# Four tokens a partition for the first four blocks of a gated-linear-attention and squared-ReLU kernel, with small array tiles and per-operation ranks

## The chip, the cores and the metric

One Trainium2 chip (trn2), one of its cores. The metric is device time in microseconds (us) of one execution. The runs of the kernel before within one job here lie 1.4 to 3.8% apart, so a comparison is always made with runs of the kernel before on the same chip in the same rounds. A run counts as slow when it is over 1.5% above the fastest run of its kernel, and else as fast. The ratio given is the mean time of one kernel's fast runs over the mean of the other's fast runs of the same rounds, with a 95% interval; it is therefore not quite the ratio of the medians quoted beside it. A "span" is the length of the one profiled execution; it is some 1.7 us shorter than that execution's time. In the views of the profile PE is TensorE (PEld its weight loads), DVE VectorE, ACT ScalarE, POOL GpSimd and SP SyncE; L701 is line 701 of that run's kernel.

## The reference

```python
def _attn_ref(q, k, v, alpha):            # (4, 8, 768, 48) each
    state = zeros((B, H, D, D))
    for t in range(S):
        state = alpha[:, :, t, :, None] * state + einsum('bhd,bhe->bhde', k[:, :, t], v[:, :, t])
        y[:, :, t] = einsum('bhd,bhde->bhe', q[:, :, t], state)

def _moe_ref(x, w_in, w_out, s, b):       # x (3072, 384), w_in (384, 2048), w_out (2048, 384)
    h = x @ w_in
    g = s * maximum(h, 0) ** 2 + b
    return g @ w_out
```

The attention runs over 24 blocks of 128 tokens. For each block there are a cumulative sum of log alpha, scores under a mask, a state product and the output of the block (`y`). Then come the first product (`h`), ReLU, square, and the second product. The constant `b` becomes one row, b times the column sums of `w_out`, which a small "bias matmul" makes once all of `w_out` has landed; the second product's results cannot be finished before.

## The kernel before

A small list scheduler orders all operations from modelled durations and ranks, and they are emitted in that order, so each engine has a fixed row of work. The parts that matter here:

```python
    h_ps = [ps.tile([128, 512], FP32, name=f"h_ps{i}") for i in range(2)]     # two tiles
    o_ps = [ps.tile([128, 512], FP32, name=f"o_ps{i}") for i in range(2)]
...
    def mm1(w):                                  # one unit of the first product
        hp = h_ps[w % 2]
        for i, j in enumerate(js):
            for kk in range(3):
                nc.tensor.matmul(out=hp[:, i * n : (i + 1) * n],
                                 lhsT=w_in_bf[:, kk, 128 * j : 128 * (j + 1)],
                                 rhs=xd_sb[g % 3][:, kk, 0:n], start=(kk == 0), stop=(kk == 2))

    def relu(w):
        nc.scalar.activation(out=r_sb[w % 2], in_=h_ps[w % 2], func=AF.Relu)
...
    def st_yevac(n):                             # output of a block, PSUM to the input of the first product
        dst, src = xd_sb[g % 3][:, :, t * C : (t + 1) * C], y_of(n)
        if n < 2 * NR2:                          # blocks loaded as pairs: tokens come in another order
            dst = dst.rearrange("a k (p j) -> a k j p", j=2)
            src = src.rearrange("a k (j p) -> a k j p", j=2)
        nc.scalar.activation(out=dst, in_=src, func=AF.Copy)
...
    def fill(idle, at):                          # keeps TensorE active in the gaps that the model sees
        for _ in range(int((idle - FILL_GAP) / (0.44 if at < COLD else 0.22))):
            nc.tensor.matmul(out=o_ps[0], lhsT=zeros[:, 0:128], rhs=zeros, start=True, stop=True)
```

While TensorE fills one `h_ps` tile (a named buffer; `ps` lies in PSUM, where TensorE writes its results), ScalarE reads the other.

## Time and profile before

| | before |
|---|---|
| time, median (range) of the 4 runs beside the changed kernel | 188.42 us (186.82 to 189.61) |
| span of the profiled execution | 183.4 us |
| first matmul of the first product | 16.99 us |
| end of the bias matmul | 38.33 us |
| rest of the span after it | 145.1 us |

The last two rows are the sum that the prediction works with. The prediction shows the page, the windows and the chain. Three groups, with shapes kept apart: line, engine, operation, tiles, shapes and count; then busy us and mean ns of one; then the engine's idle time just before and what ended it.

```profile
L692 PE MATMUL h_ps<-xd,w_in_bf 128*128 128x256 bf16 x528 | 67.7, 273 | 0.1
L701 ACT ACTIVATE r<-h_ps 128x512 bf16<-128x512 f32 x96 | 56.3, 604 | 30.3 <-PE h_ps L692 22.8 <-DVE gt L707 3.6 <-DVE am L498 1.2
L672 ACT ACTIVATE xd<-o_ps 128x384 bf16<-128x384 f32 x2 | 1.2, 600 | 1.8 <-PE o_ps L527 1.8
```

The chain (start, us, what):

```profile
131.72 0.34 PE py_ps L527 x16
132.06 1.42 PE h_ps L692 x12
133.48 0.65 PE o_ps L754 x4
```

### The profile page before, as it was taken

Reading aid. Unit: us, or ns where it says so; the run is one execution under the profiler, and the core shown is the slowest. Engines: PE = TensorE matmul, PEld = TensorE weight load, DVE = VectorE, ACT = ScalarE, POOL = GpSimd, SP = SyncE. Lnnn points to the kernel's source line nnn. Section 1 sums busy time; section 2 is a strip of 40 time slices with the busy share of each in tenths; the row PEclk is TensorE's granted clock in tenths of the full one; section 3 lists DMA queues with packets and bytes.
Section 4 is the critical chain, followed back from the end, with each engine's and each line's share of the span. In section 5 each row is a group of like instructions: output and inputs, shape, how many; then the busy total and the mean of one; then the engine's idle time right before and its main releaser. Section 6 shows DMA issues by size and latency. Waiting matters only on the chain.

```text
span 183.4 us, 5324 instructions
## 1 busy us (share of the span) xinstructions
PE 174.6 (95%) x2133; PEld 124.2 (68%) x2135; DVE 138.7 (76%) x255; ACT 106.0 (58%) x215; POOL 40.2 (22%) x70
## 2 busy tenths in 40 slices
PE   6988896999999999999999999999999999999993
PEld 2356574767777776676776776776876776777762
DVE  2377999999899898687789688577897788544421
ACT  3437699946676565674764754853753662665400
POOL 7995032022112423110303311101230131000000
PEclk9999999999999999999999999999999999999999
DMA  5999999999999999996998979996974994101112
GB/s 154 355 295 321 361 370 323 193 178 223 201 185 199 214 183 192 205 211 156 228 169 178 211 153 215 185 228 146 210 175 103 209 194 119 46 4 43 43 43 86
DMA packets 115816, 34.42 MB, mean 188 GB/s; under 512 B 109008, under 2 KB 114256, under 8 KB 115792
## 3 DMA queue, kind: packets, MB, share of 16 engines
q1 hardware_dynamic: 98832, 29.89, 69.2%
q10 hardware_dynamic: 16896, 4.20, 15.7%
q8 instruction: 16, 0.26, 0.6%
q14 instruction: 8, 0.07, 0.1%
q0 software_dynamic: 64, 0.00, 0.0%
HBM read 25.17 MB, written 4.72 MB: 163 GB/s over the span
## 4 chain that ended last, share of the span: by engine, by line
PE 79%; DVE 8%; SPq 6%; DMA 4%; issue 1%; DVEq 0%
PE o_ps L754 32%; PE h_ps L692 31%; PE py_ps L527 5%; SPq L217 5%; PE a_ps L489 4%; DMA gt<-in_k_dram 4%; PE ct_ps L386 2%; DVE colpart L342 2%; DVE gt L707 1%; SPq L309 1%; PE ct_ps L447 1%; PE ct_ps L433 1%; DVE colsum L347 1%; DVE qk L589 1%; PE o_ps L723 1%
## 5 line engine op out<-in xcount | busy, mean ns | idle before, releaser
L692 PE MATMUL h_ps<-xd,w_in_bf 128*128 128x256 bf16 (+1 forms) x624 | 74.4, 265 | 0.1
L701 ACT ACTIVATE r<-h_ps 128x512 bf16<-128x512 f32 x96 | 56.3, 604 | 30.3 <-PE h_ps L692 22.8
L754 PE MATMUL o_ps<-w_out_bf,gt 128*128 128x384 bf16 x368 | 69.5, 326 | 1.4 <-ACT w_out_bf L318 1.3
L692 PEld LDWEIGHTS <-w_in_bf 128*128 128x128 bf16 x624 | 55.1, 97 | 11.1 <-issue 0.4
L707 DVE TENSOR_TENSOR gt<-r 128x512 bf16<-128x512 bf16 x96 | 42.7, 456 | 19.5 <-ACT r L701 18.4
L754 PEld LDWEIGHTS <-gt 128*128 128x128 bf16 x368 | 34.6, 98 | 19.4 <-issue 1.5
L498 DVE TENSOR_TENSOR am<-a_ps,mask 128x1024 bf16<-128x1024 f32 x24 | 29.3, 1221 | 2.3 <-PE a_ps L489 2.0
L483 POOL TENSOR_TENSOR s_st<-s_st,blast 128x384 bf16<-128x384 bf16 x16 | 14.6, 914 | 63.7 <-DVE s_st L472 46.0
L410 POOL CAST vp<-v_in 128x384 bf16<-128x384 f32 x20 | 12.2, 608 | 47.7 <-DMA v_in<-in_v_dram 40.7
L672 ACT ACTIVATE xd<-py_ps 128x384 bf16<-128x384 f32 x22 | 11.0, 502 | 17.8 <-PE py_ps L527 15.9
L765 DVE SCALAR_TENSOR_TENSOR o_sb<-o_ps,s_col,bias_w 128x384 f32<-128x384 f32 x23 | 14.2, 616 | 6.0 <-PE o_ps L754 5.0
L380 ACT ACTIVATE la<-a_in 128x384 bf16<-128x384 f32 x20 | 10.4, 521 | 7.3 <-DVE gt L707 4.5
L416 DVE TENSOR_TENSOR qk<-q_in,b_s 128x384 bf16<-128x384 f32 x20 | 12.5, 627 | 0.8 <-ACT b_s L402 0.7
L421 DVE TENSOR_TENSOR qk<-k_in,binv 128x384 bf16<-128x384 f32 x20 | 11.9, 596 | 0.1
L402 ACT ACTIVATE b_s<-ct_ps 128x384 f32<-128x384 f32 x20 | 9.7, 486 | 2.6 <-PE ct_ps L386 2.2
L405 ACT ACTIVATE binv<-ct_ps 128x384 f32<-128x384 f32 x20 | 9.9, 495 | 0.0
L489 PE MATMUL a_ps<-qkT 64*128 64x128 bf16 x192 | 9.5, 219 | 0.4 <-DVE am L498 0.2
L489 PEld LDWEIGHTS <-qkT 64*128 64x128 bf16 x192 | 5.5, 94 | 6.5 <-issue 5.1
L1026 PE MATMUL o_ps<-zeros 128*128 128x512 bf16 x19 | 7.7, 551 | 1.3 <-DVE zeros L235 1.3
L527 PE MATMUL py_ps<-am,vp 128*32 128x128 bf16 x352 | 8.8, 219 | 0.0
L472 DVE TENSOR_TENSOR s_st<-ct_ps,s_st 64x192 bf16<-64x192 f32 x20 | 7.0, 352 | 2.0 <-PE ct_ps L447 1.6
L527 PEld LDWEIGHTS <-vp 128*32 128x32 bf16 x384 | 6.5, 97 | 0.9 <-issue 0.6
(95 smaller groups left out, 133.4 us busy)
## 6 DMA issues: line engine op xcount, KB each, us to landing
out_dram<-o_sb SPq DMA_DIRECT2D x23, 192.0 KB, 2.5
v_in<-in_v_dram SPq DMA_DIRECT2D x20, 192.0 KB, 3.8
a_in<-in_alpha_dram SPq DMA_DIRECT2D x20, 192.0 KB, 4.1
k_in<-in_k_dram SPq DMA_DIRECT2D x20, 192.0 KB, 4.0
q_in<-in_q_dram SPq DMA_DIRECT2D x20, 192.0 KB, 3.9
wst<-in_moe_w_in_dram SPq DMA_DIRECT2D x4, 768.0 KB, 7.5
gt<-in_moe_w_out_dram SPq DMA_DIRECT2D x4, 768.0 KB, 9.2
gt<-in_alpha_dram SPq DMA_DIRECT2D x2, 384.0 KB, 4.9
```

What stands on the lines that cost most here:

```text
L410: nc.gpsimd.tensor_copy(out=vp_sb[n % 4].rearrange("a p (x d) -> a p x d", d=D)[:, :, 0:3:2, :], in_=v_in[n % NIN].rearrange("a (p e) d -> ...
L416: nc.vector.tensor_tensor(out=qk_sb[n % 4][:, 0, :, 0:D], in0=q_in[n % NIN], in1=b_sb[n % 2], op=ALU.mult)
L421: nc.vector.tensor_tensor(out=qk_sb[n % 4][:, 1, :, 0:D], in0=k_in[n % NIN], in1=binv_sb[n % 2], op=ALU.mult,)
L483: nc.gpsimd.tensor_tensor(out=s_sb[n % 3], in0=t1_sb[n % 2], in1=bl, op=ALU.mult)
L489: nc.tensor.matmul(out=a_ps[:, e, p, :], lhsT=qkT[64 * e : 64 * e + 64, 1, p, :], rhs=qkT[64 * e : 64 * e + 64, 0, p, :], start=True, stop ...
L498: nc.vector.tensor_tensor(out=am_sb[n % 2].rearrange("a e p t -> a (e p) t"), in0=a_ps.rearrange("a e p t -> a (e p) t"), in1=(mask2 if n ...
L527: nc.tensor.matmul(out=y_of(n)[32 * (x % 4) : 32 * (x % 4) + 32, x // 4, :], lhsT=(st[:, p, c0 : c0 + 32] if e is None else vp[:, p, c0 + ...
L692: nc.tensor.matmul(out=hp[:, i * n : (i + 1) * n], lhsT=w_in_bf[:, kk, 128 * j : 128 * (j + 1)], rhs=xd_sb[g % 3][:, kk, 0:n], start=(kk = ...
L701: nc.scalar.activation(out=r_sb[w % 2], in_=h_ps[w % 2], func=AF.Relu)
L707: nc.vector.tensor_tensor(out=gt_sb[:, s0 : s0 + m, js[0] : js[0] + len(js)].rearrange("a s j t -> a j s t"), in0=r, in1=r, op=ALU.mult,)
L754: nc.tensor.matmul(out=op[:, 0:d_model], lhsT=gt_sb[:, s0, j], rhs=w_out_bf[:, j, :], start=(j == 0), stop=(j == NJ - 1),)
L765: nc.vector.scalar_tensor_tensor(out=ots, in0=o_ps[(x // 4) % 2][:, 0:d_model], scalar=s_col, in1=bias_w, op0=ALU.mult, op1=ALU.add,)
```

## The change

Intent: the first four blocks, which before were loaded as two pairs with two tokens a partition (384-byte pieces), are loaded as one quad with four tokens a partition (768-byte pieces). V is brought into order by 32-row array tiles, the state products of these blocks run on 32 rows, and every early operation has a rank of its own. `NPE` is the number of blocks that TensorE transposes; the others go to transposing DMAs. The core of the diff (the table of some 200 ranks, renamings and the scheduler's bookkeeping are cut):

```diff
-GROUPS = [2, 2, 1, 1, 2, 2, 2, 2, 2, 2, 2, 2, 2]
+GROUPS = [2, 2, 2, 2, 2, 2, 2, 2, 2, 2, 2, 2]
-NPE = 8
+NPE = 6
...
-TC2 = ["DVE", "DVE"]
-CE = ["POOL", "DVE", "ACT", "ACT", "ACT", "ACT", "ACT", "ACT"]
+R = 4
+TC2 = ["ACT", "ACT", "ACT", "DVE"]
+A2 = [0, 1, 0, 0]
+CE = ["POOL", "ACT", "DVE", "POOL", "ACT", "POOL", "ACT", "ACT"]
...
-    h_ps = [ps.tile([128, 512], FP32, name=f"h_ps{i}") for i in range(2)]
+    hh_ps = ps.tile([128, 2, 512], FP32, name="hh_ps")
+    h_ps = [hh_ps[:, i] for i in range(2)]
...
+            in_=src[0, :, 0 : R * C, :].rearrange("h (s j) d -> s h (j d)", j=R),
...
+    def a_of(n):
+        return hh_a if n < R and A2[n] else a_ps
...
+    def quad_vshift(c):                  # 4 matmuls on 32 x 32 array tiles a block
+            nc.tensor.matmul(out=v4_ps[c][RC * j : RC * j + RC, 0 : H * D], lhsT=ident_bf[r, r], ...
+                tile_position=(RC * c, RC * j))
...
     def st_yevac(n):
+        if n < R:
+            dst = dst.rearrange("a k (p j) -> a k j p", j=R)
+            src = src.rearrange("a k (j p) -> a k j p", j=R)
...
     def fill(idle, at):
-        for _ in range(int((idle - FILL_GAP) / (0.44 if at < COLD else 0.22))):
+        for _ in range(int((idle - FILL_GAP) / (0.11 if at < COLD else 0.06))):
-                out=o_ps[0], lhsT=zeros[:, 0:128], rhs=zeros, start=True, stop=True
+                out=o_ps[0][:, 384:512], lhsT=zeros[:, 0:128], rhs=zeros[:, 0:128], start=True, stop=True
```

The two lines with `hh_ps`: during the start-up the same tile (the "two-bank tile" of the expectations, which call 512 FP32 columns a bank) also serves, as one view, for cumulative sums and for one block's scores.

## The prediction

> **What bounds the kernel now.** I read the page first (busy shares, 40 slices), then a table of windows, then the chain that ended last, then the groups with shapes kept apart, from which all durations below come.
>
> ```profile
> PE   6988896999999999999999999999999999999993
> DVE  2377999999899898687789688577897788544421
> DMA  5999999999999999996998979996974994101112
> GB/s 154 355 295 321 361 370 323 193 178 223 201 185 199 214 183 192 205 211 156 228 169 178 211 153 215 185 228 146 210 175 103 209 194 119 46 4 43 43 43 86
> ```
>
> One slice is 183.4/40 = 4.585 us. TensorE looks full nearly everywhere, but in the first eight slices that is partly filler and gaps. So I cut the span where the work changes:
>
> ```profile
> 10.00:18.00 8.00, 6.59 (x116) 4.64 (x115) 6.29 (x10) 4.62 (x9) 5.77 (x10) 1.00 1.03 305
> 18.00:28.00 10.00, 8.97 (x121) 6.49 (x120) 9.76 (x16) 8.42 (x14) 1.50 (x2) 1.00 1.07 366
> 28.00:38.30 10.30, 8.90 (x89) 6.18 (x89) 10.19 (x19) 9.83 (x17) 1.00 (x1) 1.00 0.99 237
> 38.30:60.00 21.70, 21.70 (x356) 16.25 (x354) 20.46 (x38) 13.50 (x33) 4.39 (x7) 1.00 0.97 201
> 60.00:100.00 40.00, 40.00 (x502) 28.73 (x499) 33.87 (x65) 23.95 (x54) 8.72 (x11) 1.00 1.13 194
> ```
>
> Columns: window, length, then busy us and count of PE, weight loads, DVE, ACT and POOL, granted clock, DMA share, GB/s. From 18 to 38.3 VectorE (9.76 of 10, 10.19 of 10.3) and, in its second half, ScalarE (9.83) have no room, while TensorE has holes. From 38.3 on TensorE is full. The chain says the same:
>
> ```profile
> 11.76 6.75 DMA gt<-in_k_dram
> 19.08 1.82 DVE qk L589 x2
> ...
> 29.46 1.50 DVE colpart L342
> ...
> 34.48 0.87 DVE colpart L342
> ...
> 36.83 0.54 DVE colsum L350
> 37.41 0.91 PE o_ps L367 x2
> 38.33 0.65 PE h_ps L692 x6
> ```
>
> Columns: start, us, what. The K load of the second pair landed at 18.5; then VectorE in one run to the last fold of the column sums at 37.4; then the bias matmul; then TensorE alone to 180.35, and about 3 us for the last two stores. So the model is: span = (end of the bias matmul) + (TensorE work ordered after it) + (its small gaps) + 3.05.
>
> Check of that model on this kernel. In program order after the bias matmul stand 74 first-product units of 6 x 256 columns and 8 of 12 x 128 (0.65 and 0.67 us each in the chain), 88 second-product quads (0.65; the last four run as a split tail of 2.66), 20 score groups (0.33), 17 + 20 output parts (0.17 and 0.34), 4 transposes (0.45), 19 cumulative sums (0.17) with 15 last-row parts (0.18), 16 state products (0.17). That is 140.3 us. Measured: 180.35 - 38.33 = 142.0. The model leaves 1.7 us of gaps in all the rest.
>
> [...] its granted-clock column stays at 1.00: the first 384-column matmuls, at 5.0 us, start 0.3 apart; the same four at 16.1 us start 0.165 apart. [...] The pair loads move 384 B pieces, yet the second slice, all pairs, shows 355 GB/s against 361 and 370 in the slices of 1.5 to 2 KB weight rows: at most 4% to win on 3.1 MB. [...] The before kernel has 64-row products (0.34 us for eight) beside full ones and shows no gap that I can assign to it.
>
> **The change part by part.** (1) Two pairs become one quad. Per-instruction work on the muls is unchanged: 4 of 128x768 before (0.95 to 1.1), 4 now. Four pair transposition copies on DVE at 0.68 become one on DVE and three on ACT. An ACT pass costs 0.81 at 768 and 1.48 at 1536 columns, so 1.04 at 1024 (estimate). DVE saves 3 x 0.68 = 2.0, ACT pays 3.1. (2) V moves: four ACT copies at 0.48 before, four at about 0.50 now; the 32-row matmuls replace two 0.35 blocks with four, and state products double from 8 to 16 pieces (0.34 to about 0.7 each block). TensorE is idle then. (3) Weight casts move: of eight, before ACT 6, DVE 1, POOL 1; now ACT 4, DVE 1, POOL 3. ACT saves 2 x 1.48 = 3.0, what (1) costs it. (4) Blocks 6 and 7 go to DMA transposes: TensorE saves 2 x 0.45, DVE 2 x 0.69; two more transposing DMAs. (5) Groups of one block vanish (0.1 us). (6) New order: before the bias matmul there are now 13 first-product units instead of 14, but also one transpose, one more cumulative sum, score group and state product. Summing the new order as above, 138.8 us stand after the bias matmul: 140.3 - 138.8 = 1.5 us less, 0.9 of it from (4).
>
> Everything now hangs on when the bias matmul ends. Walk through the new order with the durations above:
>
> - Loads. The transfers ran at about 0.36 MB/us from 2.5 us. Alpha is now 0.79 MB, so it lands at about 5.0 (4.1 before); Q 7.2, K 9.3, V 11.5, then the eight weight pieces of 0.79 MB: 13.7, 15.9, 18.1, 20.3, 22.4, 24.6, and after block 4's inputs 29.0 and 31.2.
> - Logs in two halves: 5.1 to 6.75. Twelve of sixteen cumulative matmuls, partly at half rate: to about 8.5. Four exponentials of 0.81: to 11.8. Muls from 9.5, the last ends at 13.3 (K waits for nothing).
> - Transposes to 14.5; ACT copies 13.5 to 16.7; four V copies to 18.7. First score group at 17.5, first mask 17.95 to 19.2, first-product matmuls from about 23 (17.0 before), as the ACT cast of the second weight piece (landing 20.3) stands ahead of block 1's output copy.
> - DVE from the first mask to the fold: 4 masks 4.9, 3 state adds 2.2, bones 0.7, three column parts 2.9 and three adds 2.9, ten squares 4.2, block 4's two muls 1.1 and copy 0.7, fold 0.55: 20.2 us in a row, 38.0. ACT from the first output copy at 20.1 to the eleventh relu: 4 copies 2.4, 4 casts 5.9, 11 relus 6.3, two logs 1.0, exponentials 1.2, about 17 to 18: 37 to 38, and the unit before the bias matmul waits for that relu.
>
> So the fold or that unit is done at about 38.3 and the bias matmul ends near 39.0, against 38.33: 0.7 later with 1.5 us less left. Span 39.0 + 138.8 + 1.7 + 3.05 = 182.6 against 183.4, -0.5%. I shade it to -0.7%, since the ranks per operation were evidently searched for and my walk takes every queue as rigid and every wait in full.
>
> **Rivals.** A: the gain is real and larger. If the quad lets DVE and ACT run with fewer waits (the DMA moved only 295 and 321 GB/s in slices three and four, where 360 would bring 0.45 MB more, or 1.3 us), the last weight lands earlier and the fold comes at 36.5: span about 180, -1.8%. For it: VectorE waits 5.3 us for the first exponential and the second pair's K only lands at 18.5. Against: 20 us of DVE work after the first mask do not shrink. B: the whole is a wash or a loss. The first product starts 6 us later, and ACT, which has as much work as before, has it in a row; a cold clock through all sixteen cumulative matmuls (0.32 each) adds 1.3 us to all after it. Bias end 40.5: span 184, +0.4%. C: DMA becomes the bound between 40 and 60. Its share there is already 0.97, loads run without a pause at the SP, and two transposing DMAs (queue ten: 15.7% of the span for 16, so 1.8 us each) come in just then. Against: no TensorE wait on inputs after 40. If it bit, +1 to +2 us.
>
> **Range and chances.** The recorded median is 189.01 with runs from 186.82 to 189.61, some 1.5% apart, and the profiled execution took 185.12. 189.0 x 0.993 = 187.7. The mechanism gives -1.8% to +0.6%, the scatter of medians of such runs adds about 1 us: 185.3 to 189.6. Over 2% faster would need rival A in full and favourable scatter: 0.14. Over 2% slower needs B and C together: 0.06. Within 2%: 0.80.
>
> **What would show it.** Right: in the windows VectorE and ScalarE still full from about 20 to 38, the chain running through DVE or ACT lines to the fold or a relu, the bias matmul ending at 38 to 40, then TensorE full for about 140.5 us; one transposition copy in DVE and three in ACT near 1.04 us; quad loads not visibly faster per byte; first product after 22. Wrong: bias end before 37 (rival A), or holes in TensorE after 40 with la or qk waiting for inputs (C), or cumulative matmuls at 0.3 spacing to the last (B). If TensorE's time after the bias matmul differs from 140.5 by more than 1.5 us, the model of fixed work and 1.7 us of gaps is wrong.

The "at most 4%" is an estimate from 355, 361 and 370 GB/s. "Half rate" in the walk and "cold clock" in rival B stand for the 384-column matmuls that start 0.3 us apart at 5.0 us and 0.165 at 16.1 us; why they do is not shown, as the clock column has 1.00 for both, and the 1.3 us of rival B are an estimate from these spacings.

## More of the kernel before

A window in the steady part (columns as in the prediction: busy us and count of PE, weight loads, DVE, ACT, POOL, then clock, DMA share, GB/s):

```profile
80.00:100.00 20.00, 20.00 (x252) 14.39 (x249) 16.52 (x33) 11.56 (x26) 3.81 (x5) 1.00 1.00 190
```

TensorE is busy for all 20 us.

The source contains no waits between engines: they are put in when it is built.

## The result, and the profile after

| | before | after |
|---|---|---|
| time, median (range), 4 runs each | 188.42 us (186.82 to 189.61) | 206.06 us (205.27 to 208.1) |
| ratio of the fast runs, 95% interval | | 1.096 (1.084 to 1.108) |
| span | 183.4 | 206.4 |
| first matmul of the first product | 16.99 | 28.04 |
| end of the bias matmul | 38.33 | 46.47 |
| rest of the span after it | 145.1 | 159.9 |

The kernel became 9.6% slower; the prediction said 0.7% faster, with 0.06 for slower by over 2%. Of the 23 us between the spans, 8.1 lie before the end of the bias matmul and 14.9 after it, where the prediction had seen at most the 1 to 2 us of its rival C.

The page of the changed kernel (tenths of 40 slices, 5.16 us each):

```profile
PE   7898999799999699899989989989988988888894
PEclk9999559999999999999999999999999999999999
```

TensorE now has 8s all the way (and a 6 where it had 9s), and in slices five and six (20.6 to 31.0 us) the granted clock was half. The windows:

```profile
18.00:28.00 10.00, 9.42 (x167) 7.38 (x166) 7.73 (x11) 5.22 (x9) 5.62 (x5) 0.61 0.96 306
28.00:38.30 10.30, 9.76 (x106) 7.14 (x105) 6.46 (x12) 7.47 (x13) 1.70 (x3) 0.88 1.00 260
80.00:100.00 20.00, 18.62 (x236) 13.08 (x234) 14.02 (x29) 11.70 (x26) 2.57 (x4) 1.00 0.93 170
120.00:140.00 20.00, 17.96 (x231) 13.00 (x230) 12.81 (x25) 10.37 (x22) 2.67 (x4) 1.00 0.89 173
```

In the kernel before, VectorE had 9.76 of 10 us from 18 to 28; here it has 7.73, so it is not the bound, and the mean clock is 0.61. In the steady part TensorE lacks 1.4 and 2.0 us in each 20. The chain says what it waits for:

```profile
136.15 1.48 PE hh_ps L760 x12
137.63 0.02 issue
137.65 1.09 ACT r L769 x2
138.75 0.04 issue
138.79 1.25 PE hh_ps L760 x10
```

Two units run (12 matmuls without a break), then the first product stands for 1.1 us while both relus run, then the next two units start. TensorE fills the first 0.8 us of that with scores and output parts and is idle for the last 0.34. ("issue" is time in which an engine waited for nothing that the profile shows.) The whole run has 26 such waits, the longest of 1.6 us. Before, the second unit's matmuls covered the first one's relu. The groups agree:

```profile
L760 PE MATMUL hh_ps<-xd,w_in_bf 128*128 128x256 bf16 x576 | 74.3, 275 | 13.8 <-ACT r L769 13.5
L769 ACT ACTIVATE r<-hh_ps 128x512 bf16<-128x512 f32 x96 | 53.3, 594 | 49.9 <-PE hh_ps L760 44.0 <-DMA qkT<-qk 2.3 <-DVE gt L775 2.1
L740 ACT ACTIVATE xd<-o_ps 128x384 bf16<-128x384 f32 x2 | 2.1, 1028 | 3.7 <-PE o_ps L590 3.7
```

First row: 13.5 us in which TensorE was released by a relu; nothing of the kind before. Second row: the relu itself is as fast as before (594 against 604 ns), but waits 44.0 instead of 22.8 us for TensorE. Third row: the output copy of a quad's block takes 1.03 us, where a pair's took 0.60; the prediction had taken 0.6.

The start-up, as a timeline (start, us, engine, line, operation, count; in brackets idle time before and its releaser):

```profile
18.52 0.22 PE L1084 MATMUL o_ps<-zeros 128*128 128x128 bf16 x1 [0.94 <-ACT vp L712]
...
20.69 1.45 PE L721 MATMUL ct_ps<-vc,qk 32*128 32x96 bf16 x16
...
28.04 2.65 PE L760 MATMUL hh_ps<-xd,w_in_bf 128*128 128x256 bf16 x12
```

A filler, meant to keep TensorE active, waited itself for 0.94 us: it writes into `o_ps[0]`, which at that moment holds a V move that ScalarE has not copied yet. The filler's columns (384 to 511) are not those of the V move (0 to 383): here too two parts of one tile waited for each other. Two us later 16 state products take 1.45 us, where the 16 ahead of them had taken 0.85, and the first product starts at half clock: 12 matmuls in 2.65 us instead of 1.48.

So there are three suspects (the shared tile, the half clock, the copies), and the walk's own figures. The trace has one more, weaker sign for the first: at the line of the 96 relus ScalarE's queue had 92 separate semaphore instructions before, and 55 after; what each of them waited for is not shown.

### The profile page after: what moved, and what is told of

Its sections match the earlier page's. It is cut to its first block, busy times and chain, and to the rows that moved or that the text cites. A ratio compares the mean times of both kernels' runs of the same rounds, so it can differ in the third digit from the quotient of the medians.

```text
span 206.4 us, 5426 instructions
## 1 busy us (share of the span) xinstructions
PE 185.6 (90%) x2215; PEld 134.1 (65%) x2215; DVE 134.8 (65%) x252; ACT 106.9 (52%) x215; POOL 42.1 (20%) x73
## 5 line engine op out<-in xcount | busy, mean ns | idle before, releaser
L760 PE MATMUL hh_ps<-xd,w_in_bf 128*128 128x256 bf16 x576 | 74.3, 275 | 13.8 <-ACT r L769 13.5
L769 ACT ACTIVATE r<-hh_ps 128x512 bf16<-128x512 f32 x96 | 53.3, 594 | 49.9 <-PE hh_ps L760 44.0
L822 PE MATMUL o_ps<-w_out_bf,gt 128*128 128x384 bf16 x368 | 70.4, 326 | 0.0
L775 DVE TENSOR_TENSOR gt<-r 128x512 bf16<-128x512 bf16 x96 | 43.6, 463 | 34.6 <-ACT r L769 32.9
L561 DVE TENSOR_TENSOR am<-a_ps,mask 128x1024 bf16<-128x1024 f32 x23 | 28.1, 1222 | 3.5 <-PE a_ps L552 3.2
L740 ACT ACTIVATE xd<-py_ps 128x384 bf16<-128x384 f32 x22 | 11.9, 543 | 15.7 <-PE py_ps L590 12.6
L468 POOL CAST vp<-v_in 128x384 bf16<-128x384 f32 x20 | 11.1, 555 | 38.0 <-DMA v_in<-in_v_dram 37.9
L530 DVE TENSOR_TENSOR s_st<-ct_ps,s_st 64x192 bf16<-64x192 f32 x30 | 10.6, 353 | 7.4 <-PE ct_ps L505 7.0
L474 DVE TENSOR_TENSOR qk<-q_in,b_s 128x384 bf16<-128x384 f32 x20 | 11.4, 568 | 2.6 <-ACT b_s L460 2.5
L1084 PE MATMUL o_ps<-zeros 128*128 128x128 bf16 x113 | 9.8, 259 | 2.2 <-DVE zeros L295 1.3
L1084 PEld LDWEIGHTS <-zeros 128*128 128x128 bf16 x113 | 8.7, 118 | 1.7 <-DVE zeros L295 1.2
(103 smaller groups left out, 142.2 us busy)
```

Of the source, the lines that this page charges most:

```text
L474: nc.vector.tensor_tensor(out=qk_sb[n % 4][:, 0, :, 0:D], in0=q_in[n % NIN], in1=b_sb[n % 2], op=ALU.mult)
L561: nc.vector.tensor_tensor(out=am_sb[n % 2].rearrange("a e p t -> a (e p) t"), in0=a_of(n).rearrange("a e p t -> a (e p) t"), in1=(mask4 if ...
L760: nc.tensor.matmul(out=hp[:, i * n : (i + 1) * n], lhsT=w_in_bf[:, kk, 128 * j : 128 * (j + 1)], rhs=xd_sb[g % 3][:, kk, 0:n], start=(kk = ...
L775: nc.vector.tensor_tensor(out=gt_sb[:, s0 : s0 + m, js[0] : js[0] + len(js)].rearrange("a s j t -> a j s t"), in0=r, in1=r, op=ALU.mult,)
L822: nc.tensor.matmul(out=op[:, 0:d_model], lhsT=gt_sb[:, s0, j], rhs=w_out_bf[:, j, :], start=(j == 0), stop=(j == NJ - 1),)
L1084: nc.tensor.matmul(out=o_ps[0][:, 384:512], lhsT=zeros[:, 0:128], rhs=zeros[:, 0:128], start=True, stop=True)
```

## The experiments

My theory: the shared tile causes nearly all of what happened after the bias matmul, as the accesses to both halves are ordered as accesses to one thing; the half clock and the copies cause part of the rest. Rivals: the changed order or the 32-row work disturb the steady part; or the half clock does the damage by delaying everything. There were 14 runs (kernels, with 4 or 6 timed executions each), in six jobs; each job had its own runs of the kernel before, whose median was 184.79, 185.89, 187.55, 187.17, 186.55 and 189.17 us. "Bias end" is the end of the bias matmul, "rest" the span after it. All runs passed the comparison with the reference; three of them with a defect that is told below.

| run | time, median | ratio to before | 95% interval | bias end | rest |
|---|---|---|---|---|---|
| b_onetile | 205.0 | 1.112 | 1.104 to 1.119 | 38.3 | 165.0 |
| b_npe6 | 187.96 | 1.012 | 1.005 to 1.019 | 38.9 | 148.1 |
| a_pool | 189.94 | 1.026 | 1.020 to 1.033 | 43.3 | 144.8 |
| a_warm | 188.16 | 1.013 | 1.002 to 1.025 | 42.5 | 143.9 |
| a_evac | 190.19 | 1.024 | 1.019 to 1.029 | 43.5 | 145.3 |
| a_warm2 | 186.88 | 1.005 | 1.002 to 1.008 | 41.6 | 143.4 |
| a_both | 186.47 | 1.005 | 1.000 to 1.011 | 41.1 | 143.6 |
| a_both8 | 190.86 | 1.015 | 1.009 to 1.022 | 43.5 | 146.4 |
| a_tc | 186.67 | 0.995 | 0.989 to 1.000 | 40.8 | 143.4 |
| a_cast | 187.69 | 1.006 | 1.000 to 1.012 | 43.0 | 143.7 |
| a_cast_sh | 204.03 | 1.096 | 1.089 to 1.103 | 42.8 | 159.0 |
| a_fix | 187.03 | 1.006 | 1.000 to 1.012 | 41.5 | 143.9 |
| a_slim | 186.39 | 1.001 | 0.996 to 1.007 | 40.4 | 143.7 |
| a_last | 190.42 | 1.020 | 1.014 to 1.026 | 43.6 | 144.1 |

### b_onetile: the shared tile alone, in the kernel before

```diff
-    h_ps = [ps.tile([128, 512], FP32, name=f"h_ps{i}") for i in range(2)]
+    hh_ps = ps.tile([128, 2, 512], FP32, name="hh_ps")
+    h_ps = [hh_ps[:, i] for i in range(2)]
```

> The kernel before with one edit: the two PSUM buffers of the first product become two halves of one two-bank tile, as the change has them. Theory (one tile makes one dependency, so that the pair of buffers no longer alternates: TensorE waits for both relus before it fills either half): 6 to 10% slower than before, 199 to 207 us; most of the loss lies after 40 us, where TensorE falls from 20.0 busy of 20 to 18 to 19, and the waits list TensorE waiting for the relu by some 10 to 15 us in total where before shows none. Rival (the loss comes from the quad start and the clock that dips there; [...] sharing a tile costs nothing): within 1% of before, no such waits.

Measured: 11% slower, with the bias matmul at 38.3 as before and all 20 us in the rest. Windows, then waits (engine, line, released by, us in total, times, longest):

```profile
80.00:100.00 20.00, 18.11 (x222) 13.17 (x211) 13.93 (x27) 10.59 (x26) 1.98 (x3) 1.00 0.87 169
120.00:140.00 20.00, 17.63 (x226) 12.03 (x224) 12.21 (x22) 8.83 (x21) 1.01 (x2) 1.00 0.69 146
```

```profile
PE hh_ps L693 <- ACT r L702: 16.8, 28, 1.0
PEld L693 <- issue: 22.7, 36, 1.2
```

The clock is 1.00 and nothing else is changed, and yet TensorE has the same holes and the same releaser. The two lines alone, then, cost as much as the whole change lost.

### a_pool: the changed kernel with two tiles from the first product on

```diff
-    hh_ps = ps.tile([128, 2, 512], FP32, name="hh_ps")
-    h_ps = [hh_ps[:, i] for i in range(2)]
+    start_ps = ExitStack()
+    hp = start_ps.enter_context(tc.tile_pool(name="hp", bufs=1, space=bass.MemoryType.PSUM))
+    hh_ps = hp.tile([128, 2, 512], FP32, name="hh_ps")
+    ...
+    def split_h():                       # called ahead of the first unit of the first product
+        start_ps.close()
+        hq = ctx.enter_context(tc.tile_pool(name="hq", bufs=1, space=bass.MemoryType.PSUM))
+        h_ps[:] = [hq.tile([128, 512], FP32, name=f"h_ps{i}") for i in range(2)]
```

> The changed kernel with the same instructions in the same order on every engine, but from the first first-product matmul on its two PSUM buffers are two tiles again, in the place of the two-bank tile of the start. Theory of the shared tile: most of the loss goes, 186 to 192 us (ratio 0.985 to 1.02 of before), TensorE full again after 50 us, relus waiting for TensorE one by one. What is left against before is the start: a bias matmul that ends at 42 to 46 instead of 38.3, of which the half clock between 20 and 30 us is part. Rival (the start or the groups or the two more transposing DMAs cause it): still 203 to 207.

The start-up still has its two-bank view; each engine's row of instructions is the same as in the changed kernel. Measured: ratio 1.026 instead of 1.096, rest 144.8 instead of 159.9.

```profile
L779 ACT ACTIVATE r<-h_ps 128x512 bf16<-128x512 f32 x96 | 55.3, 598 | 29.0 <-PE h_ps L770 17.6 <-PE ct_ps L513 2.9 <-DVE s_st L538 2.5
```

The relus wait 17.6 us for TensorE again (22.8 before, 44.0 after). The changed order and the 32-row work are thereby cleared of the loss in the steady part. The half clock stays (0.50 from 18 to 28 us in this run too), and so do 2.6%.

### a_warm and a_warm2: fillers that do not wait

```diff
+            warm(WARM_N)                 # 20 fillers into a_ps after the V moves, in place of the one that waited
+        if n < 2:                        # a_warm2 only
+            warm_o(WARM_Y)               # 12 after the outputs of blocks 0 and 1
+        warm_o(WARM_M)                   # a_warm2 only: 10 ahead of the first unit
```

> As a_pool, and in addition 20 filler matmuls right behind the V moves, into a bank that nothing waits for, in place of the one filler that waited 0.9 us for a V copy. Theory of the clock (the granted clock falls to one half at 20 us [...] and that doubles every matmul until 30 us): the granted clock stays at 1.00 from 18 to 30 us, first-product matmuls start 2 to 4 us earlier than in a_pool, and the time is 1 to 3 us below a_pool. Rival (the start is bound by the loads, VectorE and ScalarE, and a slow TensorE hides behind them): the clock stays up and the time is within 0.7 us of a_pool.

> As a_warm, with more filler: 12 matmuls behind the outputs of blocks 0 and 1 each and 10 ahead of the first first-product matmul. In a_warm the half clock came back from 24.9 to 28.3 us, so that the first 12 first-product matmuls took 2.69 us instead of 1.48. If clock is what a_warm still loses: granted clock 1.00 all the way from 18 to 38 us, first units 1.2 us shorter, bias matmul 0.7 to 1.5 us earlier than the 42.5 of a_warm, time 0.5 to 1.5 us below it. If the filler itself stands in the way or ScalarE bounds: same or slower by up to 1 us.

Measured: in its profiled execution a_warm had the half clock later, from 24.9 us, rather than not at all (two of its four runs had a mean clock of 1.00):

```profile
24.86 2.69 PE L785 MATMUL h_ps<-xd,w_in_bf 128*128 128x256 bf16 x12 [0.65 <-ACT xd L763]
```

With the fillers of a_warm2 the clock was 1.00 throughout, 12 such matmuls took 1.47 us, the bias end fell from 43.3 to 41.6, and the ratio from 1.026 to 1.005. In one job, a_evac and a_both (below), which differ only in the fillers, had 1.024 and 1.005. Fillers and clock change together here; both together were worth about 2%. The dip is not the changed kernel's alone: in the first job five runs of the kernel before had a mean clock of 1.00 and took 184.3 to 185.6 us, and two, which count as slow, had 0.972 and 0.973 and took 187.3 and 189.4; all four runs of the changed kernel had 0.973 to 0.975. From 17.0 to 20.2 us, just before the clock fell, TensorE was busy for 2.21 of 3.2 us in the changed kernel, with no single wait over 0.94; in a_warm2 it was busy for 2.95. That alone does not tell when the clock falls: the kernel before was busy for 1.99 of the 3.41 us from 27.28, and its clock stayed at 1.00. What makes it fall is not shown.

### a_evac and a_both: output copies that write in order

```diff
-            dst = dst.rearrange("a k (p j) -> a k j p", j=R)
-            src = src.rearrange("a k (j p) -> a k j p", j=R)
+            dst = dst.rearrange("a k (p j) -> a k p j", j=R)
+            src = src.rearrange("a k (j p) -> a k p j", j=R)
```

> As a_pool (two first-product tiles again), but the output copies of the first four blocks walk the tokens in the order of their destination, so that they write side by side and read PSUM in strides; in a_pool they write every fourth element and take 1.02 to 1.12 us each, against 0.49 for an ordinary block and 0.60 for the pairs of before. If the strided write is what costs, these four copies fall to about 0.5 us, ScalarE has 2 us less to do before the bias matmul, and the time is 0.5 to 2 us below a_pool (188 to 189.5). If a strided read costs as much, 1.0 us each as before and the same time.

> a_warm2 and a_evac together. If the two terms add and with the shared tile make up the whole loss: bias matmul ends at 39 to 41 us, and the time is within 1% of before (0.985 to 1.005). If something else in the quad start still costs: 1.01 or more.

Now the copy reads PSUM with the stride and writes in order:

```profile
L748 ACT ACTIVATE xd<-o_ps 128x384 bf16<-128x384 f32 x2 | 1.0, 481 | 3.7 <-PE o_ps L598 3.7
```

0.48 us instead of 1.03. So the stride in the write cost (every fourth element 1.03 us, every second 0.60 in the kernel before), and a stride of 32 FP32 elements in the read, with the write in order, did not. But a_evac's time is that of a_pool (1.024 and 1.026), and a_both's that of a_warm2. My expectation missed: the copies were 1.7 times as long as I had costed, and nothing on the path waited for the 2.2 us that the four save.

### b_npe6 and a_both8: the number of blocks transposed on TensorE

```diff
-NPE = 8                 # b_npe6, in the kernel before
+NPE = 6
-NPE = 6                 # a_both8, in a_both
+NPE = 8
```

> The kernel before with one constant: blocks 6 and 7 are transposed by DMA, as in the change. My sum says that TensorE has 0.9 us less to do after the bias matmul: 0.3 to 1.0 us below before. Rival (the two more transposing DMAs fall into 38 to 60 us, where the DMA share is 0.97, and delay the inputs): 1 to 2 us above before, with TensorE waits on inputs after 40 us.

> The previous variant (own tiles, all fillers, copies that write in order) with blocks 6 and 7 transposed on TensorE again (NPE 8 instead of 6). If the loss of 2 to 3 us that NPE 6 showed in the kernel before is what two more transposing DMAs cost at this stage, the stretch after the bias matmul falls from 143.6 to about 141.5 us, and the ratio to the kernel before is 0.993 to 0.998. If that loss came from an order whose ranks were chosen for NPE 8, the ranks here were chosen for 6: then TensorE only has 0.9 us more to do (2 x 0.45), the stretch becomes about 144.5 and the ratio about 1.01.

Each kernel lost about 1% when it got the other's value: the rest grew from 145.1 to 148.1 in the one and from 143.6 to 146.4 in the other. In that stretch TensorE was busy for 142.2 us in b_npe6, where the kernel before has 142.0: no work was saved, and the loss is gaps. In a_both8 it was busy for 141.9 us, where a_both has 140.5: 1.3 us more work, and the rest gaps. So neither fixed price fits both, not the 0.9 us that I had credited to NPE 6, nor a cost of two more transposing DMAs. The likely reading, not tested, is that the value goes with the ranks, which move the whole order when it changes. What in the order costs it stays open. Both profiles also show a dip of the clock in the start-up (a_both8's to 0.7 in its fifth slice), but three of b_npe6's four runs and five of a_both8's six had a clock of 1.00. b_npe6's line:

```profile
PEclk9965999999999999999999999999999999999999
```

### a_tc, a_cast, a_cast_sh: what holds the first product; and the tile once more

```diff
-TC2 = ["ACT", "ACT", "ACT", "DVE"]
+TC2 = ["ACT", "DVE", "ACT", "DVE"]                       # a_tc
+        begin[at["cast_w_in 1 1"]] = begin[at["st_yevac 1"]] + 1e-6      # a_cast, from a_tc: one swap in ScalarE's row
-WARM_M = 10                                              # and fewer fillers ahead of the first unit
+WARM_M = 4
-        h_ps[:] = [hq.tile([128, 512], FP32, name=f"h_ps{i}") for i in range(2)]
+        hq_ps = hq.tile([128, 2, 512], FP32, name="hq_ps")               # a_cast_sh: a_cast, one tile again
+        h_ps[:] = [hq_ps[:, i] for i in range(2)]
```

> The same variant with NPE 6, and two of the four transposition copies on VectorE (one before): ScalarE then has two copies of 1.03 us in a row instead of three. If that row delays the first product, the first score group comes about 0.7 to 1 us earlier than 17.86, the first product about as much earlier than 25.5, the bias matmul ends near 40.2 instead of 41.06, and the ratio to the kernel before is 1.000 instead of 1.0054. If the arrival of the second weight piece (its cast on ScalarE waited for the transfer until 22.4 and stands ahead of block 1's output copy) sets the first product, nothing moves: first product 25.5, bias end 41, ratio 1.005.

> The variant with two transposition copies on VectorE, and on ScalarE one swap: block 1's output copy before the cast of the second weight piece, which waited for its transfer until 22.4 us; and 4 fillers instead of 10 ahead of the first product. If that cast is what held the first product at 25.4, the copy starts near 22.3, the first product near 24.2 (minus 0.4 for the fillers, about 0.8 for the copy), the bias matmul ends near 39.6 instead of 40.76, the span is near 183.0 and the ratio to the kernel before about 0.988. If the third unit then waits for the later cast, or the rest of TensorE's queue (state products, output parts) fills the time, the bias end stays near 40.7 and the ratio near 0.9945.

> Exactly that kernel with one word of allocation changed: the two hidden tiles are again two halves of one tile of two banks, as in the changed kernel, but with all the other remedies kept. If the shared tile alone carries the loss, also in the changed kernel's order, the stretch after the bias matmul grows from about 143.5 to 160 to 165 us and the ratio to the kernel before is 1.09 to 1.11. If the other defects (half clock, copies with a stride) were needed for the loss, it is under 1.05.

Measured: in a_tc the first scores came 1.5 us earlier (16.4 against 17.9) but the first product only 0.3 (25.2 against 25.5); the row of ScalarE copies was not what held it. In a_cast_sh, whose order is a_cast's, block 1's output copy started at 22.80 straight after its product, and the first product still at 25.30: the weight cast was not it either. (a_cast's own profile had a late start, told below, and its first product at 27.1.) Both expectations of an earlier first product missed. That a_tc's ratio, 0.995, came out better than the 1.000 expected is not explained by 0.3 us.

a_cast_sh is the clean control of the main point: the same kernel but for the tile, in the same rounds, one window each, a_cast first:

```profile
60.00:100.00 40.00, 40.00 (x497) 28.58 (x495) 31.80 (x63) 23.30 (x54) 7.29 (x11) 1.00 1.04 197
```

```profile
60.00:100.00 40.00, 38.19 (x473) 26.66 (x472) 30.37 (x58) 21.75 (x49) 5.75 (x9) 1.00 0.96 177
```

Rest 143.7 with two tiles and 159.0 with one, at a clock of 1.00 in both: the loss does not need the half clock.

A defect of mine in these three: with the new order the 20 fillers came to stand after the first score group, in whose last head they write. Block 0 loses one head's own part, and the comparison with the reference let it pass. In a_tc the first mask also waited 0.61 us for these fillers. The times are those of the instruction streams as they ran, and a_cast and a_cast_sh have the same stream, but none of the three is a kernel to use.

Another thing showed here. a_cast and a_tc start with the same instructions, and yet a_cast's first exponential came at 10.84 us and a_tc's at 8.78. The changed kernel's profile has the late start and a_pool's the early one; the changed kernel first:

```profile
6.65 1.44 PE L626 MATMUL hh_ps<-la,U_bf 128*128 128x384 bf16 x4 [0.95 <-ACT la L617]
...
10.42 0.81 ACT L647 ACTIVATE b_s<-a_ps 128x768 f32<-128x768 f32 x1 [3.09 <-PE a_ps L626]
```

```profile
8.73 0.81 ACT L655 ACTIVATE b_s<-a_ps 128x768 f32<-128x768 f32 x1 [1.47 <-PE a_ps L634]
```

Both have 40 fillers of 128 columns from 1.25 us on; in a_pool they took 3.88 us and the first four cumulative matmuls after them 0.81, in the changed kernel 4.45 and 1.44, and there these matmuls ran at about 0.32 us until 10 us. (The clock line shows 9s in both.) What decides which start an execution has is not shown; with the same first instructions, the first exponential came 1.7 to 2.1 us apart in two executions. A bias end of a single profile is therefore not better than 2 us, and differences of that size in the table are not to be explained.

### a_fix, a_slim, a_last: the last two microseconds

```diff
-WARM_N = 20, after the fourth V move             # a_fix, from a_tc: 12, after the third V move, so ahead of the scores
+WARM_N = 12
-WARM_Y = 12; WARM_M = 10                         # a_slim: with a_cast's swap and fewer fillers
+WARM_Y = 6; WARM_M = 4
+        begin[at["load_w_out 2 6"]], begin[at["load_w_out 3 7"]] = l4 - 2e-6, l4 - 1e-6   # a_last: l4 = start of block 4's loads
```

> In the last three variants (two transposition copies on VectorE; the swapped cast; its twin with the shared tile) the 20 fillers came to stand after the first score group and write into its last head: block 0 loses one head's own part there, which the comparison lets pass, and the first mask waited 0.6 us for them. Here the variant with two copies on VectorE has 12 fillers ahead of the first score group, so that nothing is overwritten. If the 0.6 us were on the way to the first product, it starts about 0.5 earlier than 25.2, bias end near 40.2, ratio 0.990 to 0.995. If TensorE's own row of fillers and small products sets it, it comes about 8 x 0.056 = 0.45 us earlier anyway; the half clock coming back would show as 5s in the clock line and a bias end above 42.

> The same with the swapped cast, 6 fillers instead of 12 after each of the first two output groups and 4 instead of 10 ahead of the first product: 18 x 0.065 = 1.2 us less in TensorE's row between 20 and 25 us. In the shared-tile twin, whose start was warm, the copy of block 1 came without waiting for the cast (22.8) and the first product still started at 25.3, as TensorE's row of fillers and small products had no gap: the cast was not it. If that row sets the first product, it starts near 24.0 and the bias matmul ends near 39.3, span 182.5 to 183.5, ratio 0.985 to 0.992. If the masks and state products (VectorE, GpSimd) set it, the row gets gaps instead and the first product stays near 25; [...] bias end 42 or later, ratio above 1.0.

> The variant with fewer fillers, and only the order of the load queue changed: the last two output-weight pieces ahead of block 4's four inputs instead of behind them. In the variant before, they were issued at 27.5 to 28.7 us, because the issue of block 4's inputs took 5.5 and 3.3 us, and the last landed near 35.8, straight before the final column sums; the prediction's walk had it at 31.2. If that landing sets the fold, the last pieces land 4 to 6 us earlier, the bias matmul ends at 38.5 to 39.5 instead of 40.40, and the span is 182.5 to 183.5, ratio 0.985 to 0.995. If VectorE's row sets it, or block 4 (whose inputs come later by as much) holds up the row, the bias end stays at 40 to 41 and the ratio near 1.00.

Measured: a_slim's first product started at 24.8, a_fix's at 25.6, which suggests that TensorE's own row of fillers and small products between 20 and 25 us sets part of it (a_slim also has the swapped cast, and 0.8 us is within what two executions differ by); the bias end came at 40.4 against 41.5, and the ratio is 1.001 against 1.006, which is not to be told apart. a_slim's chain runs through the last weight load:

```profile
28.25 7.59 DMA gt<-in_moe_w_out_dram
35.89 0.67 DVE qkT L527
36.56 0.86 DVE colpart L413
...
39.49 0.91 PE o_ps L438 x2
```

The last piece of `w_out` is asked for at 28.25 and lands near 35.8, where my walk had 31.2; then come the last column sums and the bias matmul. a_last moved the last two pieces ahead of block 4's inputs and changed nothing else. It was no remedy: ratio 1.020, bias end 43.6. The ratio is less sure than it looks: five of its six runs had a clock of 0.99, like the six runs of the kernel before in that job that count as slow (189.2 to 193.1 us) and are left out. Its one run at 1.00 took 189.3 us, where the kernel before's fast runs took 186.1 to 187.6. Its chain then leads through block 4's and block 5's input loads, and the clock dipped again, to a mean of 0.83 from 18 to 28 us; the stretch after that:

```profile
28.00:41.00 13.00, 11.31 (x133) 8.61 (x130) 9.27 (x18) 10.53 (x18) 2.55 (x3) 1.00 0.92 192
```

TensorE had 12.97 of these 13 us in a_cast and in a_both8; here it waits. This favours the rival of that run (block 4 holds up the row), but the clock dip mixes in. What the last 1.4 us of the bias end consist of stays open.

None of the 14 kernels is shown to beat the kernel before. The best correct one, a_slim, is level with it (1.001, 0.996 to 1.007). a_tc is lower (0.995) but computes one head of block 0 wrong, and its mended twin a_fix is at 1.006.

## Why the prediction was wrong

By its own steps:

1. "The model leaves 1.7 us of gaps in all the rest." This is the step that failed. It was measured on the kernel before and carried over unasked, though the diff changed what those gaps depend on: two tiles became one, a line that the prediction's list of six parts leaves out. In the changed kernel the rest is 159.9 us, where 138.8 + 1.7 + 3.05 = 143.6 was predicted, and 11.9 us of it are waits of TensorE for relus. b_onetile shows the effect alone (rest 145.1 to 165.0), a_pool takes it away (144.8), a_cast and a_cast_sh do so once more (143.7 and 159.0). The prediction had even named the test: "If TensorE's time after the bias matmul differs from 140.5 by more than 1.5 us, the model of fixed work and 1.7 us of gaps is wrong." But none of its three rivals was about this; rival B put the loss in the start-up, rival C in the loads.

2. "1.5 us less" of work after the bias matmul: right once the tile is split. a_warm2 and a_both have 143.4 and 143.6 against the predicted 143.6 and against 145.1 before. In that stretch TensorE was busy for 140.5 us in a_both and 142.0 in the kernel before, which is the 1.5. That "0.9 of it" comes from NPE 6 is not confirmed: the other value costs 1% in either direction.

3. "The bias matmul ends near 39.0": it ended at 46.5. The walk took the clock as full after the start, and the first product at about 23; it started at 28.0, and at 25.5 in a_both. The 7.5 us can be split only roughly, as each profile's start is uncertain by 2 us. Taking the half clock away, by fillers, gave 1.7 (43.3 to 41.6, a_pool to a_warm2); the ratios of the timed runs confirm the sign (1.026 to 1.005, which is more than 1.7 us). From the changed kernel to a_pool it is 3.2, of which the late first exponential explains 1.7 by the reading above and the shared tile at most the rest; these two were not separated by a run. What is left is 2.6, of which a_slim removes 1.2. The walk's landing of the last weight (31.2) was some 4.6 us too early by the landing in a_slim: it used 0.36 MB/us throughout, while the changed kernel moved 306 and 260 GB/s from 18 to 38 at a DMA share near 1. (The blocks' inputs come there, in 192-byte pieces, among the weights; whether that lowers the rate was not tested.)

4. Rival B had the right two pieces for the start-up, the cumulative matmuls at 0.32 us and the late first product, and sized them at 1.5 us together. The slow start alone is 1.7 to 2.1 us at the first exponential when it happens, and the half clock at 20 to 30 us was not in it.

5. Sizes: transposition copies on ScalarE 1.02 to 1.03 us (estimate 1.04) and V copies 0.51 to 0.55 (0.50) were right. Output copies were 1.03 instead of 0.60: the pair's duration was taken for another stride. It happened to cost nothing, as a_evac shows. The quad loads were not faster per byte (327 GB/s from 5 to 10 us, 355 in the second slice before), as predicted.

6. "VectorE and ScalarE still full from about 20 to 38": wrong, VectorE had 7.73 of 10 us; TensorE, with 9.42 of 10 at a mean clock of 0.61, was the busy one.

7. Two of its sums are off, without weight for the outcome: 182.6 against 183.4 is -0.4%, not -0.5%, and rival A's fold at 36.5 gives, with the prediction's own terms, a span near 181, not 180.

## What to carry to other kernels

Whether the work on two buffers overlaps was decided here by how they are declared: two buffers in one tile cost 7 to 11% in the three pairs of kernels that differ in it, and the remedy is to give the two-bank view its own tile and lifetime and the double buffer two tiles. In a diff, a changed declaration of a double buffer is to be costed as waits on its use (in the changed kernel 26 waits for relus, 13.5 us). And a filler has to be free of waits itself: the one here waited 0.94 us. That fewer fillers are better, as they stand in the row that they keep busy, is likely but not shown: a_slim and a_fix are not to be told apart.
